# Log decays summed by TensorE, a shorter mish, and two chunks loaded into MoE buffers, in a fused recurrence and MoE kernel

## The chip, the cores and the metric

The kernel runs on one core of a Trainium2 chip. The metric is device time in microseconds (us). Three runs of the kernel before gave 531.81, 533.33 and 534.49; their median, 533.33 us, is what a later time is compared with.

## The reference: what is computed

A gated linear recurrence feeds a mixture-of-experts style MLP with one expert:

```
f = 1.0 / (1.0 + np.exp(-f_logit))
state = f[:, :, t, :, None] * state + einsum('bhd,bhe->bhde', k[:, :, t], v[:, :, t])
y[:, :, t] = einsum('bhd,bhde->bhe', q[:, :, t], state)
...
h = x @ w_in
sp = np.where(h > 20.0, h, np.log1p(np.exp(np.minimum(h, 20.0))))
g = h * np.tanh(sp)
return (g @ w_out)
```

q, k, v and f_logit are (4, 8, 768, 48) in float32: batch, heads, time, width. The outputs y of all heads form x, 3072 tokens by 384, and the MLP has 2048 hidden units. The function from h to g is mish.

## The kernel before: tiles, stages, queues

The sequence is cut into chunks of 128 time steps of one batch, 24 in all; four of them, one of each batch, make a group of 512 tokens. In a chunk the recurrence becomes matmuls: k is divided and q multiplied by the running product of the decays f, scores are q times k under a causal mask, and a state of each batch is carried on. `prep` makes the running product: Exp on ScalarE (L351), plus one (L352), a scan on VectorE (L354, a running product of 1+exp(-f_logit)), Ln and Exp on ScalarE (L357, L358), and products on VectorE (L273, L362) or, for k, on GpSimd (L273). `attn0` to `attn3` are scores and mask (L385, L391), the transposition of k (L410), the state's update (L427, L444, L446) and the outputs (L462, L474), which are copied as a high and a low part into xt (L500, L505 or L507). Three small DMAs (L513) then move a quarter of the rows within xt.

The MLP works in units: one group of 512 tokens by one block of 128 hidden columns, 6 groups by 16 blocks, 96 units. A unit is nine matmuls into h (L212, `moe_in`), mish (L222 to L230), and nine matmuls into three output banks (L235, `moe_out`), two units later. Float32 operands are split into a high and a low part, which is why there are nine. Units 0 to 7 are group 0 with blocks 0 to 7, units 8 to 15 group 1 with the same blocks, units 16 to 31 the same two groups with blocks 8 to 15, then groups 2 to 5 follow. With a unit of group 0 the weights of its block are made out of raw 64-bit words (`split_w`): a DMA of 768 KB, a copy on ScalarE (L316), three steps on VectorE (L318, L319, L321), a rounding copy on ScalarE (L323) and a subtraction on VectorE (L324).

The first four chunks come before any unit. Chunks 4 to 7 are to be done by unit 4, 8 to 11 by unit 31, and the rest are spread over the later groups (`attend_goal`). Every step is given to a planner (`Plan`) with a cost, what it reads and what it writes; a list schedule made of these costs fixes the order in which the instructions stand in each engine's queue. All engines, and SP, which issues the DMAs, work through their queue in that order. Up to the first `moe_out` the planner fills TensorE's planned idle time with dummy matmuls on zeros (`idle`, L304). Inputs go to two buffers each for l (f_logit), k, q and v, used in turn by even and odd chunks; chunk 2 has to wait until chunk 0 has let go of its buffers.

At the end a flag tells whether every decay is far enough from zero; if not, a slow path, not taken here, does all again.

Of the kernel before, what the change touches and what calls it, by code (L numbers as in the profile page):

```python
# [9 lines left out]
F32 = mybir.dt.float32  # L10
# [159 lines left out]
def recurrence_moe_kernel(  # L170
# [3 lines left out]
    fl: bass.AP,  # L174
    kk: bass.AP,
# [22 lines left out]
    two = ctile([P, 1], F32, "two")  # L198
    hcap = ctile([P, 1], F32, "hcap")
# [18 lines left out]
    def mish(h, n, g, gh, gl):  # L218

        u = n  # L220
        return (
            ("act", T_ACT(GT, True, 1), 0, lambda: nc.scalar.activation(u, h, AF.Relu, bias=hcap, scale=-1.0)),  # L222
            ("act", T_ACT(GT, False, 1), 0, lambda: nc.scalar.activation(u, u, AF.Exp, bias=hcap, scale=-1.0)),  # L223
            ("dve", T_DVE(GT), 1, lambda: nc.vector.scalar_tensor_tensor(n, u, 2.0, u, ALU.add, ALU.mult)),  # L224
            ("dve", T_DVE(GT), 0, lambda: nc.vector.tensor_tensor(g, h, n, ALU.mult)),  # L225
            ("act", T_ACT(GT, False, 1), 0, lambda: nc.scalar.activation(h, n, AF.Ln, bias=two)),  # L226
            ("act", T_ACT(GT, True), 0, lambda: nc.scalar.activation(h, h, AF.Exp, scale=-1.0)),  # L227
            ("dve", T_DVE(GT), 0, lambda: nc.vector.tensor_tensor(g, g, h, ALU.mult)),  # L228
            ("act", T_ACT(GT), 0, lambda: nc.scalar.activation(gh, g, AF.Copy)),  # L229
            ("pool", T_POOL(GT), 1, lambda: nc.gpsimd.tensor_tensor(gl, g, gh.bitcast(F32), ALU.subtract)),  # L230
        )
# [8 lines left out]
    with tc.tile_pool(name="work", bufs=1) as pool, tc.tile_pool(  # L240
# [6 lines left out]
        v_ = ring("v", 2, [P, H * 64])  # L247
# [3 lines left out]
        inv = inv1[:, :, 1:]  # L251
# [9 lines left out]
        halves = [dram.tile([DM, GT], F32, tag=f"half{g}", name=f"half{g}") for g in range(2)]  # L261

# [25 lines left out]
        nc.vector.memset(gate[:, :, 0:1], 0.0)  # L288
# [39 lines left out]
        def load(n, parts):  # L328
            i = n % 2
            st = NP // parts  # L330
            for s in range(0, NP, st):
                for nm, dst, src in (("l", l_, fl), ("k", k_, kk), ("q", q_, qq)):
                    add("sp", 500, lambda dst=dst, src=src, s=s: nc.sync.dma_start(
                        dst[i][:, s : s + st], src[n][:, s : s + st]),
                        (), pairs((nm, i), range(s, s + st)), 65.5 * st)
            add("sp", 500, lambda: nc.sync.dma_start(v_[i], vn[n]), (), [("v", i)], 262)

        def prep(n, parts):
            i = n % 2

            taken[n] = b, keys = banks()
            f, k, q, end = l_[i], k_[i], q_[i], ends[:, n]
            st = NP // parts
            for s0 in range(0, NP, st):
# [15 lines left out]
                times(False, w, f[:, s], inv[:, s], dec[:, s], ki + kd, kf, port=False)  # L360
# [12 lines left out]
        def attn0(n, parts):  # L373

            k, q = k_[n % 2], q_[n % 2]
# [3 lines left out]
            sc = [x[:, 0 : NP * CH].rearrange("p (a c) -> p a c", a=NP) for x in b]  # L379

            def scores(s):
                for p in range(s, s + st):
                    for e in range(2):
                        for c in range(2):
                            nc.tensor.matmul(  # L385
                                sc[e][half(c), p, :], k[half(e), p, half(c)], q[half(e), p, half(c)], start=True, stop=True
# [388 lines left out]
```

## Time and profile before

| | before |
|---|---|
| median of three runs | 533.33 us |
| span of the profiled execution | 529.4 us |
| TensorE busy | 513.5 us (97%) |
| VectorE busy | 384.0 us (73%) |
| ScalarE busy | 415.2 us (78%) |
| GpSimd busy | 174.7 us (33%) |
| first matmul into h of units 0, 8 and 23 | 40.71, 93.00, 163.43 us |

The profiled execution's own time isn't told apart from its span; the median of the runs is 3.9 us more than the span. Engines are named PE (TensorE), PEld (its weight loads), DVE (VectorE), ACT (ScalarE), POOL (GpSimd) and SP (SyncE). A busy PE is not a useful PE: the dummy matmuls count too. Instructions that follow each other overlap on DVE and ACT by some 0.08 us, so the distance from start to start is what one costs.

### The profile page before, as it was taken

What the parts mean: (1) busy time and instruction counts of PE and PEld (TensorE: products, weight loads), DVE (VectorE), ACT (ScalarE), POOL (GpSimd) and SP (SyncE); (2) the same over time, 40 slices, a digit from 0 to 9 for tenths busy, and PEclk for the clock granted to TensorE, in tenths of its full rate; (3) what the DMA queues carried; (4) which work ended last, traced back from release to release, by engine and by line L of the source; (5) the groups of instructions that cost most, each with busy time, mean ns of one, the idle gap of its engine ahead of it and who ended that gap; (6) DMA issues with size and microseconds to landing.
All of it is one profiled execution on the core that took longest, in us unless ns stands there. A gap on an engine that the chain in (4) does not pass through costs nothing.

```text
span 529.4 us, 13158 instructions
## 1 busy us (share of the span) xinstructions
PE 513.5 (97%) x5362; PEld 409.4 (77%) x5362; DVE 384.0 (73%) x617; ACT 415.2 (78%) x746; POOL 174.7 (33%) x153
## 2 busy tenths in 40 slices
PE   8999898999998999999999999999999999999994
PEld 8788676777786877777877778777787777878783
DVE  6999999999996878785767577656574765454451
ACT  7878877798988878878887778878788786777771
POOL 2411432333233434333444333334242322222321
PEclk9999999999999999999999999999999999999998
DMA  8886445424510533131213132202131000010001
GB/s 267 273 269 202 140 141 170 164 89 146 163 56 4 170 109 114 74 105 41 63 38 110 44 118 81 61 22 90 36 125 42 2 0 31 1 59 1 1 1 63
DMA packets 23921, 48.86 MB, mean 92 GB/s; under 512 B 2800, under 2 KB 6256, under 8 KB 23856
## 3 DMA queue, kind: packets, MB, share of 16 engines
q1 hardware_dynamic: 23856, 47.98, 28.0%
q8 instruction: 42, 0.69, 0.5%
q14 instruction: 23, 0.19, 0.1%
HBM read 39.32 MB, written 6.29 MB: 86 GB/s over the span
## 4 chain that ended last, share of the span: by engine, by line
PE 72%; DVE 13%; ACT 8%; issue 3%; DMA 2%; DVEq 0%; ACTq 0%
PE h L212 32%; PE o L235 30%; DVE n L224 3%; PE at L427 2%; PE at L474 2%; PE at L462 2%; DVE g L225 2%; DVE g L228 2%; PE at L385 2%; DMA l<-fl 2%; DVE wl L324 1%; PE at L410 1%; ACT h L226 1%; DVE wt L321 1%; DVE wt L319 1%
## 5 line engine op out<-in xcount | busy, mean ns | idle before, releaser
L230 POOL TENSOR_TENSOR gl<-g,gh 128x512 fp32r<-128x512 f32 x96 | 128.8, 1342 | 265.2 <-ACT gh L229 246.9
L212 PE MATMUL h<-xt,wh 128*128 128x512 f32 x576 | 186.4, 405 | 6.5 <-DVE g L228 4.8
L212 PEld LDWEIGHTS h<-xt,wh 128*128 128x128 f32 x576 | 105.3, 189 | 35.3 <-DVE g L228 8.6
L235 PE MATMUL o<-gh,wh 128*128 128x512 f32 x288 | 115.8, 402 | 0.0
L212 PE MATMUL h<-xt,wl 128*128 128x512 f32 x288 | 114.8, 399 | 0.1
L235 PE MATMUL o<-gl,wh 128*128 128x512 f32 x288 | 114.2, 397 | 0.0
L235 PE MATMUL o<-gh,wl 128*128 128x512 f32 x288 | 113.4, 394 | 0.0
L224 DVE SCALAR_TENSOR_TENSOR n<-n 128x512 f32<-128x512 f32 x96 | 71.1, 741 | 58.0 <-ACT n L223 57.7
L228 DVE TENSOR_TENSOR g<-g,h 128x512 f32<-128x512 f32 x96 | 65.3, 681 | 40.0 <-ACT h L227 39.6
L222 ACT ACTIVATE n<-h,hcap 128x512 f32<-128x512 f32 x96 | 65.7, 685 | 35.9 <-PE h L212 35.2
L226 ACT ACTIVATE h<-n,two 128x512 f32<-128x512 f32 x96 | 66.0, 688 | 22.9 <-DVE g L225 22.8
L229 ACT ACTIVATE gh<-g 128x512 fp32r<-128x512 f32 x96 | 60.3, 628 | 24.4 <-DVE g L228 22.2
L225 DVE TENSOR_TENSOR g<-h,n 128x512 f32<-128x512 f32 x96 | 66.0, 687 | 7.6 <-POOL gl L230 1.1
L223 ACT ACTIVATE n<-n,hcap 128x512 f32<-128x512 f32 x96 | 69.1, 720 | 2.0
L212 PEld LDWEIGHTS h<-xt,wl 128*128 128x128 f32 x288 | 54.5, 189 | 13.7 <-DVE wl L324 0.5
L235 PEld LDWEIGHTS o<-gl,wh 128*128 128x128 f32 x288 | 54.1, 188 | 13.5 <-POOL gl L230 0.4
L235 PEld LDWEIGHTS o<-gh,wh 128*128 128x128 f32 x288 | 54.1, 188 | 12.7
L235 PEld LDWEIGHTS o<-gh,wl 128*128 128x128 f32 x288 | 54.1, 188 | 12.4
L227 ACT ACTIVATE h<-h 128x512 f32<-128x512 f32 x96 | 55.9, 582 | 1.6
L273 POOL TENSOR_TENSOR k<-k,inv 128x512 f32<-128x512 f32 (+1 forms) x26 | 31.8, 1225 | 65.7 <-DVE inv L354 28.6
L354 DVE TENSOR_TENSOR_SCAN inv<-gate,ones 128x516 f32<-128x516 f32 (+1 forms) x28 | 31.8, 1134 | 2.9 <-ACT gate L352 2.9
L304 PE MATMUL o<-state 128*128 128x128 f32 x200 | 28.3, 297 | 1.1 <-DVE gate L288 1.1
(97 smaller groups left out, 517.6 us busy)
## 6 DMA issues: line engine op xcount, KB each, us to landing
raw<-ww SPq DMA_DIRECT2D x16, 768.0 KB, 4.5
v<-vn SPq DMA_DIRECT2D x24, 256.0 KB, 4.1
l<-fl SPq DMA_DIRECT2D x20, 256.0 KB, 2.6
k<-kk SPq DMA_DIRECT2D x20, 256.0 KB, 2.7
q<-qq SPq DMA_DIRECT2D x20, 256.0 KB, 3.3
out<-ob SPq DMA_DIRECT2D x18, 256.0 KB, 2.1
xt<-xt SPq DMA_DIRECT2D x15, 128.0 KB, 2.2
half<-ob SPq DMA_DIRECT2D x6, 256.0 KB, 2.3
```

Source lines behind the costliest of these rows:

```text
L212: nc.tensor.matmul(h, w[:, j, a * P : (a + 1) * P], xt[:, x, a, :], start=(n == 0), stop=(n == 3 * NK - 1))
L222: ("act", T_ACT(GT, True, 1), 0, lambda: nc.scalar.activation(u, h, AF.Relu, bias=hcap, scale=-1.0)),
L223: ("act", T_ACT(GT, False, 1), 0, lambda: nc.scalar.activation(u, u, AF.Exp, bias=hcap, scale=-1.0)),
L224: ("dve", T_DVE(GT), 1, lambda: nc.vector.scalar_tensor_tensor(n, u, 2.0, u, ALU.add, ALU.mult)),
L225: ("dve", T_DVE(GT), 0, lambda: nc.vector.tensor_tensor(g, h, n, ALU.mult)),
L226: ("act", T_ACT(GT, False, 1), 0, lambda: nc.scalar.activation(h, n, AF.Ln, bias=two)),
L227: ("act", T_ACT(GT, True), 0, lambda: nc.scalar.activation(h, h, AF.Exp, scale=-1.0)),
L228: ("dve", T_DVE(GT), 0, lambda: nc.vector.tensor_tensor(g, g, h, ALU.mult)),
L229: ("act", T_ACT(GT), 0, lambda: nc.scalar.activation(gh, g, AF.Copy)),
L230: ("pool", T_POOL(GT), 1, lambda: nc.gpsimd.tensor_tensor(gl, g, gh.bitcast(F32), ALU.subtract)),
L235: nc.tensor.matmul(o, w[:, j, m * P : (m + 1) * P], x, start=(first and i == 0), stop=(last and i == 2))
L273: add("pool" if on_pool else "dve", cost, lambda: eng.tensor_tensor(dst, x, y, ALU.mult), reads, writes, port=port)
```

## The change

It has five parts.

1. Mish is computed as h*(1 - 2/((e+1)^2+1)) with e = exp(h): Exp (ACT), min and plus one in one TENSOR_SCALAR (DVE), square, Ln of half of it plus a half (ACT), Exp of the negative (ACT), minus one and times h in one step (DVE), the high part (ACT), the low part. It gives -g, and the outputs are negated or subtracted where they are read.
2. In units 0 to 23 (`EARLY`) the square is on ACT and the low part on DVE; later the square is on DVE and the low part on POOL.
3. Decays are summed as logarithms. For chunks 0 to 3 f_logit comes transposed (`ft`), and four matmuls with a triangle of ones sum it into PSUM; later chunks keep a scan on DVE, now a running sum. Two DVE products over l and the state's signs go; a cap (TENSOR_SCALAR) is added.
4. Chunks 2 and 3 load into n, g, ob and a third v buffer, which the MLP doesn't use yet. Chunks 1 to 3 are no longer cut in two halves, as chunk 0 still is.
5. `attend_goal` asks for the chunks of groups 3 and on two units sooner. `JOINED` is empty, so its branches aren't taken.

```diff
+E_CAP = 2.0**20
+JOINED = ()
+L_CAP = -40.0
+NTRI = GC
+EARLY = 24
...
+    def mish(h, n, g, gh, gl, early=False):
+
+        square = (
+            ("act", T_ACT(GT), 0, lambda: nc.scalar.activation(n, n, AF.Square)) if early else
+            ("dve", T_DVE(GT), 1, lambda: nc.vector.tensor_tensor(n, n, n, ALU.mult))
+        )
+        low = (
+            ("dve", T_DVE(GT), 1, lambda: nc.vector.tensor_tensor(gl, g, gh.bitcast(F32), ALU.subtract)) if early else
+            ("pool", T_POOL(GT), 1, lambda: nc.gpsimd.tensor_tensor(gl, g, gh.bitcast(F32), ALU.subtract))
+        )
         return (
...
+            ("act", T_ACT(GT, True), 0, lambda: nc.scalar.activation(n, h, AF.Exp)),
+            ("dve", T_DVE(GT / 2), 1, lambda: nc.vector.tensor_scalar(n, n, E_CAP, 1.0, ALU.min, ALU.add)),
+            square,
+            ("act", T_ACT(GT, False, 1), 0, lambda: nc.scalar.activation(g, n, AF.Ln, bias=half1, scale=0.5)),
+            ("act", T_ACT(GT), 0, lambda: nc.scalar.activation(g, g, AF.Exp, scale=-1.0)),
+            ("dve", T_DVE(GT), 0, lambda: nc.vector.scalar_tensor_tensor(g, g, 1.0, h, ALU.subtract, ALU.mult)),
             ("act", T_ACT(GT), 0, lambda: nc.scalar.activation(gh, g, AF.Copy)),
-            ("pool", T_POOL(GT), 1, lambda: nc.gpsimd.tensor_tensor(gl, g, gh.bitcast(F32), ALU.subtract)),
+            low,
...
+        spare = (
+            ([("n", 0), ("n", 1), ("g", 0), ("g", 1)], [*n_, *g_]),
+            ([("ob", 0), ("ob", 1), ("ob", 2), ("v", 2)], [*ob_, v_[2]]),
+        )
...
+                add("dve", T_DVE(w / 2), lambda s=s: nc.vector.tensor_scalar(
+                    f[:, s], f[:, s], L_CAP, None, ALU.max), (), kf, port=True)
+                x, kx = (f[:, s], kf) if n < NTRI else (gate[:, s, 1:], kg)
+                add("act", T_ACT(w), lambda s=s, x=x: nc.scalar.activation(x, f[:, s], AF.Exp, scale=-1.0), kf, kx)
+                add("act", T_ACT(w, False, 1), lambda x=x: nc.scalar.activation(x, x, AF.Ln, bias=ones), (), kx)
+                if n < NTRI:
+                    def sums(ps=ps, dec=dec):
+                        for p in ps:
+                            nc.tensor.matmul(dec[:, p, :], f[:, p, :], tri, start=True, stop=True)
...
                 times(n > 0, w, k[:, s], k[:, s], inv[:, s], ki, kk_)
-                add("dve", T_DVE(w), lambda s=s, dec=dec: nc.vector.scalar_tensor_tensor(
-                    dec[:, s], f[:, s], 2.0, dec[:, s], ALU.subtract, ALU.mult), kf, kd)
                 times(False, w, q[:, s], q[:, s], dec[:, s], kd, kq, port=False)
...
-                parts = 2 if n < GC else 1
+                parts = 2 if n < 1 else 1
...
-            return 3 * per + per * (u - 2 * NF + 2) // NF
+            return 3 * per + per * (u - 2 * NF + 4) // NF
```

The planner orders everything anew. Three places are shown. The first is SP's queue, from the second load of raw weights on in the kernel before, where l, k, q and v are the inputs' buffers and raw the weights' words:

```order
L314 DMA raw_111<-ww 128x1536
L333 DMA l_80<-fl 128x256
L336 DMA v_87<-vn 128x512
L333 DMA k_82<-kk 128x256 x2
L333 DMA l_81<-fl 128x256 x2
L336 DMA v_86<-vn 128x512
L333 DMA q_84<-qq 128x256 x2
L333 DMA k_83<-kk 128x256 x2
L314 DMA raw_110<-ww 128x1536
L333 DMA q_85<-qq 128x256 x2
L336 DMA v_87<-vn 128x512
```

and now, with n, g and ob as the buffers of chunks 2 and 3:

```order
L355 DMA ob_108<-ft 128x512
L355 DMA n_99<-kk 128x512
L355 DMA g_100<-qq 128x512
L336 DMA raw_111<-ww 128x1536
L358 DMA g_101<-vn 128x512
L355 DMA ob_109<-kk 128x512
L355 DMA ob_110<-qq 128x512
L336 DMA raw_112<-ww 128x1536
L355 DMA l_80<-fl 128x512
L358 DMA v_88<-vn 128x512
L355 DMA k_82<-kk 128x512
L355 DMA l_81<-fl 128x512
```

Before the last of the three xt transfers that unit 0 waits for there stand 10,368 KB in the queue before (these transfers counted) and 9,856 KB now: one block of raw weights fewer, and l of a seventh chunk more.

The second is VectorE among units 4 to 7, in the kernel before, where L224, L225 and L228 are mish and L318 to L324 the weights:

```order
L321 SCALAR_TENSOR_TENSOR wt_113<-raw_111,wt_113 128x768
L224 SCALAR_TENSOR_TENSOR n_97<-n_97 128x512
L228 TENSOR_TENSOR g_100<-g_100,h_118 128x512
L324 TENSOR_TENSOR wl<-wt_113,wh 128x768
L507 TENSOR_TENSOR xt_96<-at_115,xt_96 128x2x128
L507 TENSOR_TENSOR xt_96<-at_114,xt_96 128x2x128
L225 TENSOR_TENSOR g_99<-h_117,n_97 128x512
L318 TENSOR_SCALAR wt_112<-wt_112 128x768
L319 SCALAR_TENSOR_TENSOR wt_112<-raw_110,wt_112 128x768
```

and now, a little later in the queue, where L235, L239 and L230 are mish and L340 to L346 the weights:

```order
L239 SCALAR_TENSOR_TENSOR g_100<-g_100,h_118 128x512
L235 TENSOR_SCALAR n_99<-n_99 128x512
L340 TENSOR_SCALAR wt_114<-wt_114 128x768
L230 TENSOR_TENSOR gl_106<-g_100,gh_103 128x512
L341 SCALAR_TENSOR_TENSOR wt_114<-raw_112,wt_114 128x768
L343 SCALAR_TENSOR_TENSOR wt_114<-raw_112,wt_114 128x768
L239 SCALAR_TENSOR_TENSOR g_101<-g_101,h_119 128x512
L235 TENSOR_SCALAR n_98<-n_98 128x512
L346 TENSOR_TENSOR wl<-wt_113,wh 128x768
```

A unit has three VectorE steps in both, one of them now a TENSOR_SCALAR and one the low part. Ahead of the first mish step of VectorE's queue stand 74 steps on tiles before and 49 now.

The third is TensorE between units 1 and 2, in the kernel before, where L304 are dummies and L212 is h:

```order
L410 MATMUL at_116<-ident,k_83 128x128 x4
L304 MATMUL o_121<-state_73 128x128 x18
L212 MATMUL h_117<-xt_95,wh 128x512 x2
L212 MATMUL h_117<-xt_95,wl 128x512
L212 MATMUL h_117<-xt_95,wh 128x512 x2
L212 MATMUL h_117<-xt_95,wl 128x512
```

and now, with L326 and L217 in their place:

```order
L326 MATMUL o_122<-state_73 128x128 x11
L217 MATMUL h_118<-xt_96,wh 128x512 x2
L217 MATMUL h_118<-xt_96,wl 128x512
L217 MATMUL h_118<-xt_96,wh 128x512 x2
L217 MATMUL h_118<-xt_96,wl 128x512
L217 MATMUL h_118<-xt_96,wh 128x512 x2
L217 MATMUL h_118<-xt_96,wl 128x512
L443 MATMUL at_117<-ident,k_83 128x128 x4
L326 MATMUL o_122<-state_73 128x128 x3
```

After unit 0's matmuls the queue holds 20 dummies before (18 here, 2 earlier) and 14 now; each is run as two passes.

## Rows read from the trace of the kernel before

**Rows 1.** The page: busy share of VectorE in 40 slices of the span, in tenths; a slice is 13.2 us.

```profile
DVE  6999999999996878785767577656574765454451
```

**Rows 2.** The stretches 0 to 41, 41 to 93, 93 to 163 and 163 to 512 us: busy us of each engine (and instructions), then the granted clock of TensorE, the share of the DMA engines and GB/s.

```profile
0.00:41.00 41.00, 38.35 (x701) 34.01 (x702) 35.03 (x68) 32.90 (x85) 11.05 (x22) 1.00 0.82 266
41.00:93.00 52.00, 48.23 (x754) 37.93 (x754) 50.09 (x79) 40.83 (x74) 16.14 (x14) 0.97 0.50 163
93.00:163.00 70.00, 67.96 (x422) 52.91 (x422) 65.86 (x87) 60.44 (x98) 23.96 (x18) 1.00 0.36 117
163.00:512.00 349.00, 348.28 (x3441) 276.29 (x3442) 228.00 (x379) 275.41 (x482) 120.96 (x98) 1.00 0.18 59
```

**Rows 3.** The chain of waits that ended last, in order of time: start, us, what.

```profile
36.43 4.24 DMA xt<-xt
40.71 2.37 PE h L212 x9
...
48.74 4.02 PE o L304 x36
...
93.00 2.37 PE h L212 x9
...
163.43 2.37 PE h L212 x9
...
213.04 4.20 PE h L212 x18
...
512.21 10.52 PE o L235 x45
```

**Rows 4.** TensorE's instructions in order of time: start, us, line, what, and in brackets the idle time before and what ended it.

```profile
54.81 0.69 PE L427 MATMUL at<-v,kt 64*64 64x64 f32 x32
...
55.90 0.73 PE L212 MATMUL h<-xt,wh 128*128 128x512 f32 x2
...
58.20 0.46 PE L462 MATMUL at<-q,state 64*64 64x64 f32 x16
...
59.44 0.50 PE L235 MATMUL o<-gh,wh 128*128 128x512 f32 x1
...
64.28 1.13 PE L212 MATMUL h<-xt,wh 128*128 128x512 f32 x2 [2.05 <-DVE g L228]
...
93.00 0.71 PE L212 MATMUL h<-xt,wh 128*128 128x512 f32 x2 [1.49 <-DVE g L225]
...
102.33 0.73 PE L212 MATMUL h<-xt,wh 128*128 128x512 f32 x2 [0.67 <-DVE g L228]
...
163.43 0.74 PE L212 MATMUL h<-xt,wh 128*128 128x512 f32 x2 [1.37 <-DVE g L228]
```

**Rows 5.** The stretch 64 to 68 us, columns as in rows 2.

```profile
64.00:68.00 4.00, 3.71 (x9) 2.94 (x10) 4.00 (x7) 2.03 (x4) 1.61 (x1) 0.57 0.21 60
```

**Rows 6.** VectorE's instructions in order of time, columns as in rows 4.

```profile
45.01 0.40 DVE L391 TENSOR_TENSOR a<-at,causal 128x256 f32<-128x256 f32 x1
...
49.17 0.55 DVE L318 TENSOR_SCALAR wt<-wt 128x768 int32<-128x768 int32 x1
49.64 0.68 DVE L224 SCALAR_TENSOR_TENSOR n<-n 128x512 f32<-128x512 f32 x1
...
51.78 0.68 DVE L228 TENSOR_TENSOR g<-g,h 128x512 f32<-128x512 f32 x1
52.38 0.69 DVE L362 SCALAR_TENSOR_TENSOR at<-l,at 128x512 f32<-128x512 f32 x1
52.98 0.95 DVE L319 SCALAR_TENSOR_TENSOR wt<-raw,wt 128x768 int32<-128x768 int32 x1
53.85 0.68 DVE L273 TENSOR_TENSOR q<-q,at 128x512 f32<-128x512 f32 x1
...
58.19 1.22 DVE L354 TENSOR_TENSOR_SCAN inv<-gate,ones 128x516 f32<-128x516 f32 x1
59.33 0.66 DVE L225 TENSOR_TENSOR g<-h,n 128x512 f32<-128x512 f32 x1
```

**Rows 7.** VectorE's groups up to 163 us: line, operation, shapes, count, then busy us and mean ns of one.

```profile
L224 DVE SCALAR_TENSOR_TENSOR n<-n 128x512 f32<-128x512 f32 x23 | 19.0, 825 | 2.8 <-ACT n L223 2.5
...
L318 DVE TENSOR_SCALAR wt<-wt 128x768 int32<-128x768 int32 x16 | 13.2, 824 | 0.3 <-ACT wt L316 0.3
```

**Rows 8.** Single lines over the whole span: shortest, median and longest ns.

```profile
L318 DVE TENSOR_SCALAR wt<-wt x16: 547/708/1625, 10.0 to 149.1; 128x768 int32<-128x768 int32 x16
...
L224 DVE SCALAR_TENSOR_TENSOR n<-n x96: 658/692/1801, 46.3 to 513.7; 128x512 f32<-128x512 f32 x96
```

**Rows 9.** ScalarE's groups up to 163 us, columns as in rows 7.

```profile
L223 ACT ACTIVATE n<-n,hcap 128x512 f32<-128x512 f32 x23 | 16.6, 720 | 0.5
...
L316 ACT ACTIVATE wt<-raw 128x768 f32<-128x768 f32 x16 | 14.5, 907 | 0.5 <-DMA raw<-ww 0.2 <-DVE wl L324 0.2
...
L352 ACT ACTIVATE gate<-gate 128x512 f32<-128x512 f32 x7 | 4.4, 627 | 0.1
```

**Rows 10.** Stretches of 5 us at the start, columns as in rows 2.

```profile
0.00:5.00 5.00, 3.94 (x18) 3.94 (x19) 1.30 (x4) 3.29 (x8) 1.20 (x11) 1.00 0.59 168
5.00:10.00 5.00, 4.83 (x62) 4.46 (x60) 4.24 (x12) 4.82 (x15) 0.25 (x1) 1.00 1.09 355
...
20.00:25.00 5.00, 4.93 (x108) 4.24 (x90) 4.70 (x11) 4.71 (x16) 2.42 (x3) 1.00 0.81 266
```

More of the change, by code (lines that the diff above doesn't have):

```diff
@@ L373, in attn0, with score @@
         def attn0(n, parts):
-            k, q = k_[n % 2], q_[n % 2]
+            (_, kk_, kq, _), (_, k, q, _) = inputs(n)
             b, keys = taken[n]
             st = NP // parts
[L379 to L386, printed above, removed]
-                            )
+            joined = n in JOINED
+            off = 2 * C if joined else 0
+            sc = [x[:, off : off + NP * CH].rearrange("p (a c) -> p a c", a=NP) for x in b]
+            def score(e, c, p, start=True):
+                nc.tensor.matmul(
+                    sc[e][half(c), p, :], k[half(e), p, half(c)], q[half(e), p, half(c)],
+                    start=start, stop=True, skip_group_check=joined,
+                )
             def mask():
@@ L425, in update, with run @@
                         for e in range(2):
-                            c0 = (2 * p + e) * 64
-                            nc.tensor.matmul(
-                                u[c][half(e), p, :], kt_s[half(c), p, half(e)], v[half(c), c0 : c0 + 64], start=True, stop=True
-                            )
-            if n >= GC:
-                scores, mask, reads, writes = late[n]
-                add("pe", 1208, lambda: [update(), scores()], ["kt", ("v", n % 2)] + reads,
+                            update(p, c, e)
+            if joined:
+                score, mask, reads, writes = late[n]
+                inter, intra, more, touched, rest = attn3(n - 1, True)
+                def run():
+                    for p in range(NP):
+                        for x in range(2):
+                            update(p, 0, x, p == 0)
+                            score(1, x, p, p == 0)
+                    inter(True)
+                    intra(0, 64)
+                    for p in range(NP):
+                        for x in range(2):
+                            score(0, x, p, False)
+                            if not last:
+                                update(p, 1, x, False)
+                    intra(1, 32)
+                assert touched == writes
+                add("pe", 2250, run, ["kt", kv[0]] + reads + more, keys[:1] + writes)
+                rest()
+                mask()
+            elif n >= GC:
+                score, mask, reads, writes = late[n]
+                add("pe", 1208, lambda: [updates()] + [
+                    score(e, c, p) for p in range(NP) for e in range(2) for c in range(2)], ["kt", kv[0]] + reads,
                     list(dict.fromkeys(keys[: 2 - last] + writes)))
@@ L520, in recurrence_moe_kernel @@
+            if joined:
+                return inter, intra, reads, keys, rest
+            add("pe", 1100 if first else 1340, outputs, reads, keys)
+            rest()
         steps = (attn0, attn1, attn2, attn3)
```

215 lines of the change are left out of this document (113 added, 102 removed).

## The prediction, made before the changed kernel had run

> **What bounds the kernel now.** The page's slices come first: VectorE is at nine tenths in slices 1 to 11, up to about 160 us, and mostly at five to seven tenths from there on [rows 1]. TensorE's busy time can't show this, since its dummies count as busy. So I cut the span at 41, 93 and 163 us, where units 0, 8 and 23 begin [rows 3], and look at each stretch [rows 2]. From 163 to 512 us TensorE is busy for 348.3 of 349 us: there only fewer matmuls would help, and the change takes none away. From 512.21 us the last outputs run without a break [rows 3], so the end is TensorE's as well. What can be won lies ahead of 163 us, and the timeline of TensorE shows where: idle times of 2.05, 1.49, 0.67 and 1.37 us ahead of h, each ended by VectorE's mish [rows 4].
>
> **The start, up to the first h (40.71 us).** For chunk 0 to 3 a scan and two VectorE products go; a cap comes. VectorE was busy for 35.0 us of the first 41 [rows 2]. What now stands ahead of the first mish step, by distances from start to start [rows 6]: a 768-column step 0.87 (52.98 to 53.85), a 512-column one 0.60 (51.78 to 52.38), a TENSOR_SCALAR of 768 columns 0.47 (49.17 to 49.64), a scan 1.14 (58.19 to 59.33), a 256-column one 0.32 (45.01 to 45.33, 0.40 less the usual overlap of 0.08). There are ten weight steps of 768 (8.7), four TENSOR_SCALARs on them (1.9), two scans (2.3), twenty steps of 256 (6.4), four products of 512 (2.4) and nine caps (about 2.6): 24.3 us. VectorE therefore no longer sets the start. The matmuls that sum the decays, sixteen of 128x128, take the place of dummies and cost nothing; without that cover they would be some 2 us, by the 0.11 us of a dummy pass (4.02 us for 36) [rows 3].
>
> What is late next is the transfer. Unit 0 waits for the small DMAs within xt, the last of which took 4.24 us from issue to landing and ended just before the first h [rows 3]. They stand in one queue with the loads: 10.62 MB up to and with them before, 10.09 MB now. Up to 41 us the queue moved 266 GB/s on average [rows 2], between 5 and 25 us from 355 down to 266, 303 over the four stretches [rows 10]. Chunks 2 and 3 now have buffers of their own, so the queue is fed longer. With 0.84 MB in the first 5 us (168 GB/s) the rest, 9.25 MB, takes 26.1 us at 355, 30.5 at 303 and 34.8 at 266: the last transfer lands at 31, 35.5 or 39.8 us. I take 37.4, between the two nearer ones, because some of SP's loads still wait for chunks 0 and 1 to release their buffers, and because the weights' steps on ScalarE and VectorE stand ahead of the xt copies in their queues. **That is 3.3 us less**; the bounds are 9.7 and 0.9.
>
> **Units 0 to 7 (40.71 to 93.00 us, 52.3 us).** TensorE must do here eight units' h and six units' outputs, 14 x 2.10 us by the 4.20 for two units' h [rows 3], and of chunks 4 to 7 scores and update (54.81 to 55.90, 1.09) and outputs (58.20 to 59.44, 1.24) [rows 4]: 29.4 + 9.3 = 38.7. Of the 13.6 left, dummies are 4.5 (40 passes at 0.112), the two idle times 3.5, and 1.7 is a slow clock: right behind the idle 2.05 us the granted clock is 0.57 over 4 us, so part of that stretch ran at 1.2 instead of 2.4 GHz [rows 5], 4 x 0.43 = 1.7. The remaining 3.9 are transpositions and changes between kinds of matmul; they stay.
>
> VectorE was busy for 50.1 of the 52 us [rows 2]. Its three mish steps were 3 x 0.60 = 1.80 a unit. Now they are a TENSOR_SCALAR, a product and the low part. No float32 TENSOR_SCALAR of this shape is in the trace; its bounds are 0.60, as any other step of 512, and 0.32, two thirds of the weights' 0.47. I take 0.32: the weights' step is the same operation on 4-byte words in SBUF. So 1.52 a unit, 0.28 less, 2.2 for eight units. In three and a half chunks two products go and a cap comes: 3.5 x (1.20 - 0.32) = 3.1. And GpSimd holds VectorE up: the same TENSOR_SCALAR takes 547 ns at best and 1625 at worst, L224 658 and 1801 [rows 8], with means of 824 and 825 up to 163 us [rows 7]. That is 16 x 0.28 + 23 x 0.17 = 8.4 us above their best in the three stretches; with the low part off GpSimd some of it goes, between 0 and 3.5 us in this one, and I take 1.7. VectorE's need becomes 50.1 - 7.0 = 43.1 us.
>
> The Trainium skill ("SBUF — State Buffer", Who interferes with whom) has a rule for this: a VectorE instruction with two inputs in SBUF or in a two-port mode, and a GpSimd instruction that reads SBUF, shut each other out for a whole instruction. By that rule the low part, which has two SBUF inputs, would wait on VectorE for GpSimd's k products, at most one of them a chunk; the sum would lose about 1 us.
>
> The square goes to ScalarE in these units. A plain ScalarE step on SBUF takes 627 ns, the biased Exp that it replaces 720 [rows 9]; there are five ScalarE steps a unit in both, so ScalarE's need doesn't grow (40.8 of 52 us busy [rows 2]). The skill ("ScalarE: Activation LUTs", Rules for kernel authors) says that products belong on VectorE, not ScalarE. By it the square would stay where 0.60 us a unit is the dearer place, 4.8 us over eight units, and VectorE's need would be 47.9, again above TensorE's.
>
> So both stalls and the slow clock can go (3.5 + 1.7), and the 20 dummy instructions become 14, 4.5 x 6/20 = 1.4: **6.6 us less**, the stage being 45.7 us, TensorE's own. If the cap and TENSOR_SCALAR cost 0.60, VectorE needs 2.2 + 1.0 us more and the gain is about half.
>
> **Units 8 to 22 (93.00 to 163.43 us).** TensorE is idle here for 0.67 and 1.37 us [rows 4]; VectorE's 65.9 of 70 us [rows 2] fall by 14 x 0.28 = 3.9 and some of the blocking, so most of it goes: **1.5 us less** (bounds 0 and 2.0). From there on mish has four ScalarE steps, and VectorE still three; they lie beside TensorE, as does the sooner attention. Without that cover the three VectorE steps and the low part (1.3 us a unit) would still be shorter than a unit's 4.2 us on TensorE. I put it at 0.
>
> **The sum.** 3.3 + 6.6 + 1.5 = 11.4 us off the profiled span of 529.4, which gives 518.0. The median of the runs is 3.9 us above that span, and nothing outside it changes: 533.33 - 11.4 = 521.9 us.
>
> **The rivals.** *The queue of loads runs at its best and all stalls go:* the first h at 31 us, 9.7 + 6.6 + 2.0 = 18.3 less, 515.0 us. For it: the loads of chunks 2 and 3 no longer wait. Against: the raw weights of units 2 and 3 stand ahead of the last xt transfer and wait for VectorE's steps on units 0 and 1.
>
> *The transfer hides the relief:* queued bytes fall by only 5%, the start comes 2 us sooner, the first mish steps queue behind raw words that land later, and half of the second stage's gain goes: 2.0 + 3.3 + 0.5 = 5.8 less, 527.5 us. For it: 266 GB/s up to 41 us in a queue that is already near its best. Against: ScalarE waited only 0.2 us for raw words in all [rows 9].
>
> *It doesn't do what it says:* the TENSOR_SCALAR costs 0.60 and the blocking stays, so mish gains nothing on VectorE; the start brings 1 us and the stage 1: 531.3 us.
>
> *Slower:* ScalarE takes its queue in order, and a copy of raw words stands right ahead of the first square. In units 0 to 7 each late load would hold the square, mish, the two h banks and TensorE. The price is that of the stall in the trace, 2.05 us idle and 1.7 us of slow clock, 3.75. It decides from the fourth such stall beyond those that go: 4 x 3.75 = 15.0 against 11.4, 536.9 us. Against it stand the same 0.2 us.
>
> **How the numbers follow.** The forecast (516 to 525.5 us) has a chance of 0.55, the best case 0.18, the transfer 0.15, the change that doesn't do what it says 0.06, slower 0.06. A measurement of this kernel tells 0.5%, 2.7 us, from no change: faster is below 530.7. The first three cases make 0.88 for faster, the fourth is no change (0.06), the last slower (0.06). The range from 512 to 529 holds the forecast, the best case and most of the transfer case, and leaves out the two last and small ends, together some 2 in 10.
>
> **What would show it.** Right: the first h at 36 to 39 us, with a transfer of xt just before it; unit 8 at 81 to 85 us and unit 23 at 150 to 154; TENSOR_SCALAR on n at about 0.4 us; VectorE below 95% between unit 0 and unit 8; no stretch of low clock there; 163 to 512 us as full as now. Wrong: a first h at 40 us or later, new idle times of 2 us ahead of h ended by ScalarE's square or by raw words, TENSOR_SCALARs at 0.68 us, or stalls behind unit 24, where nothing was expected.

## The result, and the profile after

| | before | after |
|---|---|---|
| median of four runs | 532.57 us | 517.89 us (517.32 to 518.73) |
| span of the profiled execution | 529.4 us | 517.0 us |
| VectorE busy | 384.0 us | 337.9 us |
| ScalarE busy | 415.2 us | 365.0 us |
| GpSimd busy | 174.7 us | 143.3 us |
| first h of units 0, 8 and 23 | 40.71, 93.00, 163.43 us | 43.12, 93.08, 154.59 us |

The ratio of the two is 0.9725 (95% interval 0.970 to 0.975): 14.7 us less. The profiled execution of after took 518.73 us, 1.7 us more than its span. It is the slowest of the four, while the span before, with as much added, would belong to the fastest run of before (531.25); so the spans differ by less than the medians, by 12.4 us, which divide into +2.4 up to the first h, -2.3 in units 0 to 7, -8.9 in units 8 to 22 and -3.6 behind.

These are stretches of after, columns as in [rows 2]; the first and the last three answer to it, the 5-us ones to [rows 10].

```profile
0.00:36.00 36.00, 29.53 (x562) 26.22 (x562) 17.00 (x35) 22.90 (x54) 6.90 (x16) 0.91 0.73 252
...
10.00:15.00 5.00, 4.01 (x171) 3.43 (x169) 2.21 (x5) 4.14 (x9) 1.89 (x2) 1.00 1.03 400
15.00:20.00 5.00, 1.56 (x24) 1.03 (x15) 0.76 (x2) 1.53 (x4) 0.00 (x0) 0.94 1.04 399
20.00:25.00 5.00, 5.00 (x99) 4.37 (x100) 1.54 (x3) 2.55 (x6) 1.28 (x2) 0.50 0.73 253
...
43.12:93.08 49.96, 47.10 (x754) 37.73 (x753) 48.29 (x82) 45.11 (x83) 9.73 (x8) 1.00 0.56 188
...
93.00:163.00 70.00, 70.00 (x442) 57.17 (x441) 57.87 (x92) 63.40 (x104) 0.76 (x2) 1.00 0.35 114
...
150.00:500.00 350.00, 349.07 (x3544) 281.51 (x3543) 210.76 (x367) 233.58 (x418) 121.56 (x97) 1.00 0.19 59
```

From 93 to 163 us TensorE is now never idle, and GpSimd nearly always is. VectorE is busy for less than half of the first 36 us, so it doesn't set the start. In units 0 to 7 VectorE is still nearly full (48.29 of 49.96 us). New is the hole at 15 to 20 us: TensorE works for 1.56 us of 5, and the granted clock is 0.50 right behind.

TensorE's, ScalarE's and SP's instructions of after in order of time, columns as in [rows 4], show what stands in the hole and ahead of the first h, and which stalls are left.

```profile
16.34 0.34 PE L459 MATMUL at<-v,kt 64*64 64x64 f32 x7
20.00 1.01 PE L459 MATMUL at<-v,kt 64*64 64x64 f32 x25 [3.32 <-issue]
...
36.86 0.84 ACT L345 ACTIVATE wh<-wt 128x768 fp32r<-128x768 f32 x1 [2.00 <-DVE wt L343]
37.61 0.64 ACT L564 ACTIVATE xt<-at 128x256 fp32r<-128x256 f32 x2
38.14 0.93 ACT L338 ACTIVATE wt<-raw 128x768 f32<-128x768 f32 x1
38.95 0.66 ACT L569 ACTIVATE xt<-at 128x256 fp32r<-128x256 f32 x2
...
39.64 1.88 SPq L577 DMA_DIRECT2D xt<-xt  x3
...
43.12 0.71 PE L217 MATMUL h<-xt,wh 128*128 128x512 f32 x2
...
64.89 0.50 PE L217 MATMUL h<-xt,wl 128*128 128x512 f32 x1 [1.22 <-DVE wl L346]
...
82.18 0.69 PE L459 MATMUL at<-v,kt 64*64 64x64 f32 x32 [1.42 <-ACT kt L446]
```

Seven of 32 matmuls of one state update run, then nothing for 3.32 us, and no semaphore, engine or DMA is named for it: "issue" means that the engine waited for nothing that this view shows. The view of the DMA queues from 16.68 to 20.00 us shows one packet of 16 KB on a queue of instruction loads (packets, MB, share of 16 engines):

```profile
q8 instruction: 1, 0.02, 2.1%
```

It runs from 17.46 to 18.57 us; the section on loads comes back to it. ScalarE and VectorE wait in the hole as well, 4.11 and 5.49 us, for this update. The xt transfers are issued only at 39.64 us, because ScalarE waits 2.00 us for a weight step of VectorE and does a raw copy in between. The four stalls of [rows 4] are gone; in their place stand 1.22 and 1.42 us.

The chain of waits of after, columns as in [rows 3], for the hole and the tail:

```profile
16.68 3.32 issue
20.00 1.01 PE at L459 x20
21.01 2.00 PE h L381 x8
...
26.87 1.03 PE at L381 x8
...
496.56 4.12 PE h L217 x18
500.68 10.32 PE o L246 x45
```

Eight sums of decays (L381) take 2.00 us at the low clock and 1.03 at the full one. In the tail, where TensorE has nothing else to do and waits for nobody, 18 h matmuls take 4.12 us instead of 4.20 and 45 output matmuls 10.32 instead of 10.52 [rows 3]. The matmuls themselves run 2% faster: 10.32/45 is 229 ns, 10.52/45 is 234. Nothing in the five parts says why.

VectorE's groups of after up to 163 us answer to [rows 7], its lines over the whole span to [rows 8].

```profile
L235 DVE TENSOR_SCALAR n<-n 128x512 f32<-128x512 f32 x25 | 11.8, 472 | 2.9 <-ACT n L234 2.8
L340 DVE TENSOR_SCALAR wt<-wt 128x768 int32<-128x768 int32 x16 | 9.2, 578 | 0.8 <-ACT wt L338 0.6
...
L235 DVE TENSOR_SCALAR n<-n x96: 400/427/1212, 47.9 to 501.8; 128x512 f32<-128x512 f32 x96
```

The TENSOR_SCALAR on n takes 427 ns in the middle, less the overlap of 0.08 some 0.35 us a step; the forecast took 0.32. The one on the weights, whose instruction didn't change, fell from a mean of 824 ns to 578.

### The profile page after: what moved, and what is told of

It is laid out like the page before. It is cut to its first block, busy times and chain, and to the rows that moved or that the text cites. A ratio compares the mean times of both kernels' runs of the same rounds, so it can differ in the third digit from the quotient of the medians.

```text
span 517.0 us, 12741 instructions
## 1 busy us (share of the span) xinstructions
PE 500.7 (97%) x5324; PEld 407.4 (79%) x5324; DVE 337.9 (65%) x575; ACT 365.0 (71%) x659; POOL 143.3 (28%) x125
## 4 chain that ended last, share of the span: by engine, by line
PE 83%; DVE 9%; ACT 4%; issue 1%; DMA 1%; ACTq 0%; DVEq 0%
PE o L246 37%; PE h L217 35%; PE at L459 2%; PE at L537 2%; PE at L524 2%; PE at L443 2%; PE at L418 1%; DVE wt L343 1%; DVE inv L386 1%; DMA raw<-ww 1%; ACT wh L345 1%; DVE n L227 1%; DVE g L239 1%; DVE wt L341 1%; ACT wt L338 1%
## 5 line engine op out<-in xcount | busy, mean ns | idle before, releaser
L217 PE MATMUL h<-xt,wh 128*128 128x512 f32 x576 | 181.8, 397 | 0.0
L231 POOL TENSOR_TENSOR gl<-g,gh 128x512 fp32r<-128x512 f32 x72 | 98.9, 1373 | 197.2 <-ACT gh L240 153.4
L217 PEld LDWEIGHTS h<-xt,wh 128*128 128x128 f32 x576 | 106.2, 188 | 22.7
L217 PE MATMUL h<-xt,wl 128*128 128x512 f32 x288 | 112.9, 392 | 1.2 <-DVE wl L346 1.2
L237 ACT ACTIVATE g<-n,half 128x512 f32<-128x512 f32 x96 | 69.4, 723 | 57.3 <-DVE n L227 54.3
L239 DVE SCALAR_TENSOR_TENSOR g<-g,h 128x512 f32<-128x512 f32 x96 | 65.6, 683 | 63.4 <-ACT g L238 63.1
L235 DVE TENSOR_SCALAR n<-n 128x512 f32<-128x512 f32 x96 | 47.7, 497 | 57.1 <-ACT n L234 56.9
L234 ACT ACTIVATE n<-h 128x512 f32<-128x512 f32 x96 | 56.8, 592 | 34.3 <-PE h L217 33.5
L217 PEld LDWEIGHTS h<-xt,wl 128*128 128x128 f32 x288 | 54.1, 188 | 14.0 <-DVE wl L346 1.6
L238 ACT ACTIVATE g<-g 128x512 f32<-128x512 f32 x96 | 60.2, 627 | 1.9
L227 DVE TENSOR_TENSOR n<-n 128x512 f32<-128x512 f32 x72 | 54.1, 752 | 2.1
L554 POOL TENSOR_TENSOR state<-tmp,ends 128x256 f32<-128x256 f32 x20 | 14.4, 720 | 108.4 <-PE at L524 97.8
L296 POOL TENSOR_TENSOR k<-k,inv 128x512 f32<-128x512 f32 x20 | 25.8, 1289 | 36.5 <-ACT inv L392 21.0
L386 DVE TENSOR_TENSOR_SCAN inv<-gate,state 128x516 f32<-128x516 f32 x20 | 26.7, 1336 | 1.3 <-POOL k L296 1.3
```

Source lines behind the costliest of these rows:

```text
L217: nc.tensor.matmul(h, w[:, j, a * P : (a + 1) * P], xt[:, x, a, :], start=(n == 0), stop=(n == 3 * NK - 1))
L227: ("dve", T_DVE(GT), 1, lambda: nc.vector.tensor_tensor(n, n, n, ALU.mult))
L234: ("act", T_ACT(GT, True), 0, lambda: nc.scalar.activation(n, h, AF.Exp)),
L235: ("dve", T_DVE(GT / 2), 1, lambda: nc.vector.tensor_scalar(n, n, E_CAP, 1.0, ALU.min, ALU.add)),
L238: ("act", T_ACT(GT), 0, lambda: nc.scalar.activation(g, g, AF.Exp, scale=-1.0)),
L239: ("dve", T_DVE(GT), 0, lambda: nc.vector.scalar_tensor_tensor(g, g, 1.0, h, ALU.subtract, ALU.mult)),
```

## The experiments

Twelve kernels ran, one of them after, unchanged, in three sets on three chips, each beside the kernel before: medians 533.65, 533.5 and 534.59 us. After ran again in the first set alone (517.94 us), so kernels of the other two are compared with it across chips. Every edit but the three that only move tiles also makes the planner order the queues anew; where nothing but the order was changed (below), the time moved by 0.9 and 0.3 us. Two theories stood for the faster matmuls: that later tiles lie at other addresses (the new constants shift all tiles behind them; the weights wh and wl are allocated ahead of them and stay), or that TensorE's rows are the same and only what waits changed. For the rest, the parts were undone one at a time.

### Where the streamed tiles lie

The columns that a matmul streams are of xt for h, of gh and gl for the outputs. By the tiles' sizes they begin, modulo 2048 bytes of a partition, at 480 before and at 960 after. Three kernels move them and nothing else.

```diff
     flag = ctile([1, 1], I32, "flag")
+    pad = ctile([P, 1], F32, "pad")
```

> The kernel before with one more constant of 32 bytes a partition ahead of the state, so that the tiles that TensorE streams (xt, gh, gl) start at multiples of 64 bytes instead of 32 past one; no instruction moves. Theory (start address): nine matmuls of 512 columns take 2.06 us instead of 2.10, on 192 groups of nine 7.5 us, so about 525 against 532.6 (ratio 0.986). Rival (another chip, or the kernel's own work): 2.10 stays and the ratio is 1.00.

That kernel has all of them at 512. 533.95 us, ratio 1.0001 (0.9964 to 1.0038): no change.

```diff
         xt_ = ring("xt", 2, [P, 2, NP, GT], F32R)
+        (pad,) = ring("pad", 1, [P, 1])
         n_, g_ = (ring(nm, 2, [P, GT]) for nm in "ng")
```

> The changed kernel with 32 bytes put in between xt and the tiles of mish, so that xt stays at a multiple of 64 bytes and gh and gl don't. Theory (start address of the streamed tile): h stays at 2.06 us for nine matmuls, the outputs go to 2.10, 96 x 0.04 = 3.8 us more than the changed kernel, about 521.7. Rival (something else of the changed kernel makes matmuls faster): both stay at 2.06 and the time at 517.9.

xt stays at 960, gh and gl go to 992. 522.10 us, ratio 0.9772 (0.972 to 0.9823), 4.2 more than after in the same set.

```diff
     flag = ctile([1, 1], I32, "flag")
+    pad = ctile([P, 120], F32, "pad")
```

> The kernel before with 480 bytes a partition put ahead of the state, so that xt, gh and gl start where they do in the changed kernel, at 960 past a multiple of 2048 (before: 480; with the 32 bytes of before_pad: 512). No instruction moves. Theory (the address of the streamed tile sets the pace): nine matmuls take 2.06 us, about 7.5 us less than before, a ratio of 0.986. Rival (the changed kernel's work, not its addresses, sets the pace): 2.09 to 2.10 and a ratio of 1.00.

This is the kernel before with all of them at 960, as after has them. 528.93 us, ratio 0.9916 (0.989 to 0.9942): 4.6 less than before, where the pace alone had made 7.5 expected.

The chain of waits in the tail, columns as in [rows 3], first of the kernel before with the small pad (512), then with the large one (960), then of after with gh and gl at 992.

```profile
511.70 4.19 PE h L213 x18
515.88 10.47 PE o L236 x45
```

```profile
505.52 4.12 PE h L213 x18
509.64 10.32 PE o L236 x45
```

```profile
499.42 4.13 PE h L217 x18
503.55 10.51 PE o L246 x45
```

Within one kernel, the third, h runs at after's pace and the outputs at before's: it is the address of what is streamed. The rule behind it isn't found: 960 is fast, 480, 512 and 992 are not, so being a multiple of 64 bytes isn't it, and no other addresses were tried.

The large pad brings less than 192 groups x 0.04 = 7.7 us, as the timeline of TensorE in that kernel shows, columns as in [rows 4].

```profile
67.09 0.74 PE L213 MATMUL h<-xt,wh 128*128 128x512 f32 x2 [2.06 <-DVE g L229]
...
94.83 0.71 PE L213 MATMUL h<-xt,wh 128*128 128x512 f32 x2 [1.86 <-DMA xt<-xt]
...
137.07 0.74 PE L213 MATMUL h<-xt,wh 128*128 128x512 f32 x2 [1.48 <-DVE g L229]
...
165.98 0.73 PE L213 MATMUL h<-xt,wh 128*128 128x512 f32 x2 [1.66 <-DVE g L229]
```

Before unit 23 VectorE and the transfers set the pace, and a faster TensorE waits longer there: from the first h (42.88 us here) to unit 23's it is 123.1 us against 122.7 in the kernel before. Behind unit 23's it is 360.4 against 366.0, so the whole gain falls there.

### Mish and GpSimd

```diff
-EARLY = 24
+EARLY = 0
```

> The changed kernel with part 2 undone: in units 0 to 23, too, the square is on VectorE and the low part on GpSimd. Same addresses. Theory (GpSimd's low part holds VectorE up in the first 24 units): 2 to 6 us more than the changed kernel, 520 to 524, TENSOR_SCALARs and the weights' steps up to 163 us at a mean over 0.8 us. Rival (VectorE has slack, the move buys nothing): 517 to 519.

525.95 us, ratio 0.9833 (0.9787 to 0.9879): part 2 is worth 8.0 us, over half of the whole gain and more than the 2 to 6 expected. The TENSOR_SCALARs on n stayed below the 0.8 us expected (649 ns, below).

In the next kernel the square stays on ScalarE in units 0 to 23, and only the low part goes back to GpSimd.

```diff
-            ("dve", T_DVE(GT), 1, lambda: nc.vector.tensor_tensor(gl, g, gh.bitcast(F32), ALU.subtract)) if early else
+            ("dve", T_DVE(GT), 1, lambda: nc.vector.tensor_tensor(gl, g, gh.bitcast(F32), ALU.subtract)) if False else
```

> The changed kernel with the square of units 0 to 23 on ScalarE, as changed, but their low part on GpSimd again: VectorE has two mish steps in these units, GpSimd's step stays. Theory (GpSimd blocks VectorE, so the low part is what had to move): slower than the changed kernel by 2 us or more, 520 to 524, though VectorE has 0.6 us a unit less to do. Rival (VectorE's count of steps is what matters): 517 or less.

521.76 us, ratio 0.9776 (0.9726 to 0.9827). By the medians the square's move is worth 4.2 us of the 8.0, the low part's 3.8; by the ratios to before, each in its set, 3.0 and 4.0. The square was moved with the low part on GpSimd; a kernel with both on VectorE didn't run. The low part's is the odd one: it gives VectorE one instruction a unit more, and GpSimd has time to spare. VectorE's groups from 93 to 163 us, and that stretch (columns as in [rows 2]), first of this kernel, then of after, run again unchanged in another set:

```profile
L235 DVE TENSOR_SCALAR n<-n 128x512 f32<-128x512 f32 x16 | 9.9, 619 | 5.2 <-ACT n L234 5.2
L346 DVE TENSOR_TENSOR wl<-wt,wh 128x768 fp32r<-128x768 f32 x8 | 9.7, 1214 | 0.7 <-ACT wh L345 0.6
...
L340 DVE TENSOR_SCALAR wt<-wt 128x768 int32<-128x768 int32 x6 | 4.4, 739 | 0.2
...
93.00:163.00 70.00, 68.16 (x427) 54.31 (x426) 54.57 (x74) 59.84 (x99) 24.55 (x17) 1.00 0.35 120
```

```profile
L230 DVE TENSOR_TENSOR gl<-g,gh 128x512 fp32r<-128x512 f32 x16 | 11.0, 687 | 0.8 <-ACT gh L240 0.4
...
L346 DVE TENSOR_TENSOR wl<-wt,wh 128x768 fp32r<-128x768 f32 x8 | 7.6, 953 | 0.1
L235 DVE TENSOR_SCALAR n<-n 128x512 f32<-128x512 f32 x17 | 7.6, 445 | 2.8 <-ACT n L234 2.7
...
L340 DVE TENSOR_SCALAR wt<-wt 128x768 int32<-128x768 int32 x6 | 3.3, 557 | 0.5 <-ACT wt L338 0.3
...
93.00:163.00 70.00, 70.00 (x441) 57.07 (x441) 57.83 (x94) 64.64 (x107) 0.61 (x1) 1.00 0.35 113
```

The low part (L230) is 11.0 us on VectorE, yet VectorE is busy for only 3.3 us more with it: its other instructions are that much longer without it, while GpSimd works for 24.55 us beside them (619 ns against 445, 1214 against 953, 739 against 557). Single instructions of the kernel with the low part on GpSimd show that it is the overlap, columns as in [rows 4]:

```profile
111.82 0.43 DVE L235 TENSOR_SCALAR n<-n 128x512 f32<-128x512 f32 x1 [0.18 <-ACT n L234]
...
116.01 1.94 POOL L231 TENSOR_TENSOR gl<-g,gh 128x512 fp32r<-128x512 f32 x1 [1.74 <-ACT gh L240]
...
116.71 1.52 DVE L235 TENSOR_SCALAR n<-n 128x512 f32<-128x512 f32 x1
```

From 93 to 163 us the nine TENSOR_SCALARs on n that no GpSimd instruction overlaps take 430 ns at most, the seven others 869 in the mean; the product with h (L239), which reads one of its tiles from PSUM, takes 680 and 687. VectorE isn't full in this stretch (54.57 of 70 us), so the 3.8 us come by longer steps in chains of waits; which of these isn't told apart. The Trainium skill ("SBUF — State Buffer", Who interferes with whom) gives as the reason a port pair that VectorE and GpSimd lock in turn; these rows agree, and add what it costs. The Trainium skill's rule that products belong on VectorE ("ScalarE: Activation LUTs", Rules for kernel authors), whose figure is one for bf16, would have cost this kernel in float32 the square's 3.0 to 4.2 us.

Undoing both moves leaves VectorE's groups up to 163 us like this, with the stretch from 93 to 163 us and the stall of unit 4's h behind them:

```profile
L227 DVE TENSOR_TENSOR n<-n 128x512 f32<-128x512 f32 x22 | 19.4, 882 | 0.3
L341 DVE SCALAR_TENSOR_TENSOR wt<-raw,wt 128x768 int32<-128x768 int32 x16 | 19.1, 1196 | 0.1
...
L235 DVE TENSOR_SCALAR n<-n 128x512 f32<-128x512 f32 x22 | 14.3, 649 | 0.6 <-ACT n L234 0.6
...
93.00:163.00 70.00, 67.89 (x425) 53.31 (x424) 67.25 (x88) 51.28 (x84) 29.04 (x18) 1.00 0.38 126
...
67.89 1.22 PE L217 MATMUL h<-xt,wh 128*128 128x512 f32 x2 [3.65 <-DVE g L239]
```

VectorE is full again from 93 to 163 us, as in the kernel before [rows 2], though mish has the short TENSOR_SCALAR: at 649 ns in the mean it takes as long as a two-input step that nothing holds up (658 at best [rows 8]).

In the last of these, mish is as before the change, on the same engines, and everything else as after.

```diff
-            ("act", T_ACT(GT, True), 0, lambda: nc.scalar.activation(n, h, AF.Exp)),
...
+            ("act", T_ACT(GT, True, 1), 0, lambda: nc.scalar.activation(u, h, AF.Relu, bias=hcap, scale=-1.0)),
+            ("act", T_ACT(GT, False, 1), 0, lambda: nc.scalar.activation(u, u, AF.Exp, bias=hcap, scale=-1.0)),
+            ("dve", T_DVE(GT), 1, lambda: nc.vector.scalar_tensor_tensor(n, u, 2.0, u, ALU.add, ALU.mult)),
...
+            ("pool", T_POOL(GT), 1, lambda: nc.gpsimd.tensor_tensor(gl, g, gh.bitcast(F32), ALU.subtract)),
```

> The changed kernel with mish as before (part 1 and with it part 2 undone: Relu, Exp, two VectorE steps, Ln, Exp, a VectorE step, low part on GpSimd), all else as changed. Same addresses. Theory (mish on VectorE and GpSimd's blocking set units 0 to 22): 5 to 8 us more than the changed kernel, 523 to 526. Rival (the decays' part brought the gain there): 518 to 520.

529.54 us, ratio 0.9913 (0.9885 to 0.9941), more than the 523 to 526 expected. The new formula alone, without the moves, is worth 529.5 - 525.95 = 3.6 us. And this kernel, with the tiles at 960, is no faster than the kernel before with the tiles at 960 (528.9): parts 3 to 5 together bring nothing beside the old mish.

### Loads, sums and attention

```diff
-            if 2 <= n < GC:
+            if False:
```

> The changed kernel with chunks 2 and 3 loaded into the two buffers of before (part 4 undone). Theory (the deep queue of early loads delays TensorE's instructions): the wait of 3.3 us in the middle of chunk 1's update goes, and the first h comes at 41 us or sooner in spite of later loads. Rival (the early loads help, the wait comes by chance or from the program's size): the first h comes at 45 us or later, the wait stays.

513.35 us (512.33 to 515.08), ratio 0.9612 (0.9557 to 0.9668). Without the early loads the kernel is 4.6 us faster than after in the same set, and faster than both kernels. The other half of part 4 stays here: chunks 1 to 3 are not cut in two.

> The changed kernel unchanged, on the same chip as the others: 517.9 us, h and outputs at 2.06 us for nine matmuls. If the 3.3 us wait of TensorE at the start is tied to the program it is there again near 16.7 us, and the first h is at 43 us; if it is chance it is elsewhere or gone, and the first h comes near 39.

That is after, unchanged: 517.94 us, ratio 0.9702 (0.965 to 0.9755). The hole is there again, 2.83 us long. In the kernel without early loads, stretches and TensorE's timeline show less of it:

```profile
10.00:15.00 5.00, 4.66 (x173) 4.09 (x172) 2.89 (x6) 2.95 (x6) 1.85 (x2) 1.00 1.00 400
15.00:20.00 5.00, 3.71 (x56) 3.12 (x54) 3.70 (x9) 4.37 (x10) 1.24 (x2) 1.00 0.93 281
20.00:25.00 5.00, 4.72 (x93) 4.00 (x91) 2.64 (x3) 3.86 (x10) 1.45 (x2) 1.00 0.81 261
...
17.80 0.62 PE L459 MATMUL at<-v,kt 64*64 64x64 f32 x25 [1.16 <-issue]
...
41.86 0.51 PE L217 MATMUL h<-xt,wh 128*128 128x512 f32 x1 [0.60 <-DMA xt<-xt]
```

The transfers fall to 281 GB/s at 15 us instead of staying at 400, the wait at the same seven of 32 matmuls is 1.16 us, and the clock stays at 1.00. Yet the first h is no sooner, 41.86 us against 41.03 in the unchanged kernel, so the expected gain at the start didn't come. It gains later: the stalls of after at 64.89 and 82.18 us (62.80 and 80.10 in its second execution) have no counterpart there, as the stretch of units 0 to 7 shows, columns as in [rows 2]:

```profile
41.86:91.13 49.27, 49.27 (x765) 39.41 (x765) 47.29 (x81) 44.21 (x83) 9.90 (x8) 1.00 0.56 182
```

At its end one unit more has its outputs done (2.1 us), and the gap is 3.6 us by unit 32 and 3.8 at the end of the spans (511.4 and 515.2). The first of the two stalls ends with a weight step (L346), and the early loads put the weights off: VectorE begins the first block at 13.46 us without them and at 20.74 in the unchanged kernel, and by the first h it has begun five blocks and three. So the loss by the early loads is measured, and late weights are part of it; how much of it isn't told apart.

The hole can be followed through all runs. It always comes when TensorE has run 222 matmuls and 222 weight loads, whichever these are: after the seventh of the 32 in after, after the sixth or ninth where the order is another. And TensorE always goes on 1.28 to 1.43 us behind the end of a packet of 16 KB on the instruction queue q8, in all ten runs with the hole (18.57 and 20.00 us in after). Three kernels stop once more 127 matmuls and 128 weight loads later, and go on 1.30 to 1.46 us behind the end of the next such packet. So TensorE waits for its next instructions. What sets when the packet moves stays open: with early loads the transfers ran at 395 to 408 GB/s from 15 to 20 us in every kernel, and the hole was 0.79 us long in one and 3.32 in another.

Another order of all engines tells whether it is a chance of the planner's. Its cost for a DMA's latency was raised in both:

```diff
-    LATENCY = {"pe": 230.0, "act": 170.0, "dve": 160.0, "pool": 180.0, "sp": 1550.0}
+    LATENCY = {"pe": 230.0, "act": 170.0, "dve": 160.0, "pool": 180.0, "sp": 1650.0}
```

With the early loads:

> The changed kernel, with the planner told that a DMA lands 100 ns later (1650 for 1550); nothing else. The order of the queues changes, the work doesn't. Theory (the early loads cost 4.6 us in whatever order): 516 us or more. Rival (the 4.6 us between the changed kernel and the one without early loads is the luck of an order, in which some waits fall badly): the time moves by 2 us or more, to anywhere from 512 to 522.

Without them:

> The kernel without early loads (513.35 us), with the same 100 ns told to the planner. Theory (without early loads 4.6 us are won): 512 to 515. Rival (luck of the order): 516 or more.

517.03 us (0.9685, 0.9635 to 0.9735) against 513.68 (0.9624, 0.9566 to 0.9683): 3.4 us in another order, so the loss isn't that of one order. Here the kernel with early loads has neither of the two stalls, but its first h comes 1.45 us later (43.11 and 41.66 us); without them the packet ends at 14.93 us, TensorE reaches the place at 16.14, and there is no hole.

The next takes the scan for all chunks and leaves TensorE's sums out.

```diff
-NTRI = GC
+NTRI = 0
```

> The changed kernel with the decays of chunks 0 to 3 summed by the scan on VectorE, as the later chunks are, instead of by TensorE. Same addresses. Theory of the prediction (VectorE no longer sets the start: 17 of 36 us busy): four scans, 4.6 us of VectorE, are hidden and the time is 517 to 519. Rival (they stand in the chain to the first h): the first h comes 2 to 5 us later and the time is 520 to 523.

518.04 us (0.9697, 0.9643 to 0.9751): the sums bring nothing. The first h comes at 41.59 us, and the products that part 3 saves in every chunk stay saved; they were not undone alone. VectorE has the scan's 1.14 us to spare there, four times in the first 36 us of which it is busy for 17.

```diff
-            return 3 * per + per * (u - 2 * NF + 4) // NF
+            return 3 * per + per * (u - 2 * NF + 2) // NF
```

> The changed kernel with part 5 undone (chunks of groups 3 and on not two units sooner). All theories: they lie beside TensorE, 516.5 to 519, apart from what another order brings.

519.38 us (0.9744, 0.9686 to 0.9801): 1.4 more than after in another set, which its interval doesn't tell from nothing.

## Why the prediction came out as it did

The medians add up, from one kernel to the next: 533.5 before, 528.9 with the tiles where after has them (-4.6), 529.5 with parts 3 to 5 (+0.6), 525.95 with the new formula (-3.6), 521.8 with the square on ScalarE (-4.2), 517.9 with the low part on VectorE (-3.8). The last two steps go from one chip to another. The forecast was 521.9 us, in its range of 512 to 529. It went the forecast way for the main reason, mish on VectorE up to unit 23, but several terms were wrong. That the sum came so near is in part luck: the faster matmuls brought 4.6 us that no term had, and the early loads took 4.6 that no term had either. Of the signs named, the first h at 40 us or later, unit 8 at 93.08 us instead of 81 to 85 and VectorE at 97% in units 0 to 7 spoke against the working; unit 23 at 154.59 and the full clock in units 0 to 7 spoke for it.

**The start, forecast -3.3 us, measured +2.4 in the profiled executions.** The step that failed is the 37.4 us for the transfer. VectorE did stop setting the start, and the first h does come right behind an xt transfer: the last lands at 43.05 us. But the queue wasn't what it waited for. The last xt transfers were issued from 39.64 us on, behind ScalarE's wait for weight steps that VectorE itself had got to late, and landed within 3.0 us. The fall of bytes in the queue was the wrong measure: more bytes early meant a full queue at 400 GB/s, not a sooner end. The sums that "cost nothing" took 2.00 us instead of 1.03 in the stretch of low clock, but without them the time is the same. Nor is the hole shown to be what the start lost: without any the first h came at 41.66 us, with one of 2.83 us at 41.03. The start moves by some 2 us between executions, too: 40.71 us in the kernel before, 42.96 with the small pad, which changes no time; 43.12 and 41.03 in after itself. So of the +2.4 only the missing gain is sure.

**Units 0 to 7, forecast -6.6, measured -2.3,** or -4.4 if it is counted that 21 instead of 18 output matmuls of a kind, one unit more, were done by unit 8 (2.1 us). The dummies (28 instead of 40 passes, -1.3) and the slow clock (-1.7) went as forecast, and the pace gave 15 x 0.04 = 0.6. The step that failed is that both stalls go: TensorE's idle time fell from 3.8 to 2.9 us, not to nothing, since two new stalls took their place, and behind that is VectorE's need of 43.1 us; it was 48.29. By the first h VectorE had begun three blocks of weights where it had begun five before, since the first came at 22.16 us instead of 9.98 [rows 8]; the rest, some 4 to 5 us by the forecast's own costs, came on top here. The TENSOR_SCALAR at 0.32 was nearly right, and so was the end of the 2.05 us stall and its slow clock.

**Units 8 to 22, forecast -1.5, measured -8.9.** 2.1 of it is the unit done sooner, 29 groups x 0.04 = 1.2 the pace, 2.5 the idle times, and some 1.2 the outputs of one chunk [rows 4], which come later in the queue now. The last 1.9 are transpositions that come later and fewer changes between kinds of matmul; they are what is left over.

**GpSimd's blocking, forecast at 1.7 us** in units 0 to 7 plus some behind, is the mis-sized term. From 93 to 163 us alone VectorE's other instructions are some 7.7 us shorter with GpSimd idle (11.0 of low parts put on it, 3.3 of busy time more). By the forecast's own prices, 0.60 us a unit on VectorE against 1.7 us of relief, the low part's move would have lost; it gained 3.8. The rival that the blocking stays didn't come: the low part itself waited little, 704 ns in the mean up to 163 us against 687 beside an idle GpSimd. Nor did the rival that ScalarE's queue would hold the square.

**Later, forecast 0, measured -3.6.** The pace gives 148 groups x 0.04 = 5.9 here; one more chunk's outputs (1.2), its transposition and 0.6 us more of idle time take part of it back. That a tile's address sets how fast it streams wasn't in the forecast, nor in any row of before: it needs two kernels to be seen.

**What lies outside the span** was taken as unchanged at 3.9. It is 1.7 to 1.9 us in the four runs of after and at most 2.2 in any other; the 3.9 compared a span with the median of other runs.

## What to carry to other kernels

Before a gain is put down to an edit, compare the mean distance of the same matmuls where nothing waits, in the tail: new constants ahead of the big tiles can change it by 2%. GpSimd beside VectorE is not free room, and moving work onto VectorE can pay: price the other instructions' longer durations, not only the moved one. Undo each part of a change alone; here the early loads cost 4.6 us, the sums on TensorE and the sooner chunks brought nothing that could be measured, and without the early loads the kernel runs in 513.35 us.

## What the runs showed that was not expected

- Matmuls of 512 columns follow each other in 229 ns with their streamed tile at 960 modulo 2048 bytes, in 233 to 234 at 480, 512 or 992. Fast and slow stood side by side in one kernel.
- TensorE stopped for 3.32 us (0.79 to 3.10 in the other runs with early loads) within equal matmuls, always after 222 matmuls and 222 weight loads, and went on 1.28 to 1.43 us behind the end of a 16 KB packet of the instruction queue. The view that names what a wait ended with calls it "issue"; the view of the DMA queues shows the packet. What makes the packet late isn't shown.
- Behind that stop the granted clock was 0.50 over 5 us, the lower of the two levels. Behind before's idle time of 1.49 us there was no such stretch [rows 4]. The length of the stop alone doesn't decide: from 17 to 22 us the clock was 0.66 behind a stop of 1.47 us (the kernel without sums on TensorE) and 1.00 behind one of 1.34 (the square alone moved).
